# A fused retention and MLP kernel: two bursts of entry 2 taken together, and one scaling moved

## The chip, the cores and the metric

The kernel runs on one core of a Trainium2 chip. The metric is the device time of one execution in microseconds (us). The engines are named as in the profile: PE (TensorE matmuls), PEld (its weight loads), DVE (VectorE), ACT (ScalarE), POOL (GpSimd), SP (SyncE). Each engine runs its own queue in order; engines wait for one another by semaphores.

## The reference

Retention over 8 batch entries, 8 heads, 576 positions, 64 dimensions, and then an MLP with 2048 hidden units on the 4608 rows that come out:

```python
scores = (q @ k.T) / sqrt(64)
ret = scores * where(i >= j, gamma[h] ** (i - j), 0)   # gamma[h] = 1 - 2 ** (-5 - h)
x = (ret @ v)                                          # per entry and head
x = x.transpose(0, 2, 1, 3).reshape(4608, 512)
h = x @ w_in                                           # 512 -> 2048
out = (h * sigmoid(1.702 * h)) @ w_out                 # 2048 -> 512
```

q, k and v are loaded as bf16, sums are kept in f32.

## The kernel before

**Retention in steps.** Entry 0 is done on its own. Entries 1 to 7 are cut into 9 blocks of 64 positions, and three blocks make a step: `NWIDE` = 21 steps, m = 0 to 20, step m belonging to entry 1 + m // 3. So entry 2 has steps 3, 4 and 5, and step 5 has blocks 6 to 8. Heads 4 to 7 are shifted by 64 positions in k and v, so step 5 reads chunks 3 and 4 of the entry's five chunks of 128 positions.

A step needs two kinds of work on PE, all in 64x64 tiles. *In*: `score` (k times q of the step's blocks, L680) and `state` (sums of k times v, L666). *Out*: `values` (masked scores times v, L638) and `inter` (the running sums times q, L654). Between the two, DVE masks the scores into `sm` (`mask_wide`, L735), adds the sums to `zacc` (`state_wide`, L750 and L753) and a cast makes `zw` in bf16 of them, on DVE (L762) or on ACT (L759). After *out*, `evac_wide` (DVE, L724) multiplies by the decay and writes `xT`, the MLP's input.

`burst(m_out, m_in, cast)` puts *out* of one step and *in* of another on PE's queue at one place; either may be None. With both, the order is: one state, half of the values (the blocks of even number) with their `inter`, the scores, the other states, the second half of the values with theirs. The second half waits for PE's own first half. On DVE a burst queues `evac_wide(m_out)` first; with cast "DVE" then the mask, the sums and the cast; with cast "ACT" the sums, then the mask, and the cast is queued on ACT behind the next unit.

`step(m, into, cast)` is `burst(m, m + 1)` if `into` is true, else `burst(m, None)`; behind it `turn_step(m + 3)` queues transposing DMAs on SP (`turn_dma`, L572) that bring k and q of step m + 3 into `qk`, and from step 2 on loads are queued on POOL (L223, L236) for the entry three later. SP's queue also carries the DMAs of the output (L819).

`scale(m)` multiplies v by a decay factor on DVE (`scale_v`, L394): for step 3 chunks 0 and 1 of entry 2, for step 4 chunks 2 and 3, for step 5 chunk 4.

**The MLP in units.** 4608 rows make nine chunks of 512. For each, 16 units of `hidden` (four 128x512 matmuls, L771, then a GELU on ACT, L776) and 16 units of `project` (four matmuls, L804; the last of a row block is copied out by ACT, L813, and stored). Chunk 1 is done in two halves, with `hidden_half` (eight 128x256 matmuls, L788 and L794).

**The order** is written out by hand. `run(units, between)` queues the units in turn and behind unit i what `between[i]` holds. If a `step` stands behind a unit, the unit's matmuls wait, ahead of the first, for what the step's burst needs (`needs`); a `burst` named alone has no such effect. In the lines that change, `units_half(1, 1)` is 8 units, `units_o(1, (2, 3))` is 8, and `region(2, ...)` is chunk 2's 16 hidden and 16 project units.

Of the kernel before, what the change touches and what calls it, by code (L numbers as in the profile page):

```python
# [132 lines left out]
def bass_retnet_parallel__then__act_gelu_quick_kernel(  # L133
# [11 lines left out]
    with es:  # L145
# [469 lines left out]
        def needs(m_out, m_in):  # L615
            r = []
            if m_out is not None:
                b, cs = chunks(m_out)
                r += [("sm", si(m_out)), "zw"] + [("v", b % NST, c) for c in cs] + queries(m_out)
            if m_in is not None:  # L620
                b, cs = chunks(m_in)
                r += [(nm, b % NST, c) for nm in "kv" for c in cs]
                r += [("qk", (NC * b + c) % NQK, 1) for c in cs] + queries(m_in)
            return r
# [155 lines left out]
        def hidden_half(c, half, f, at, ahead=()):  # L780
            bank, key = at
            a0 = 512 * c + 256 * half
            toks = range(a0 // 64, a0 // 64 + 4)

            def fn(e):
                for i in range(2):
                    for a in range(4):
                        m = e.matmul(bank[:, 256 * i : 256 * i + 256],  # L788
                                     w_in_sb[:, a, 128 * (f + i) : 128 * (f + i) + 128],
                                     xT[:, a, a0 : a0 + 256],  # L790
                                     start=(a == 0), stop=(a == 3))
                return m
            R.op("PE", fn, r=[("w_in", f // 2)] + [("xT", x) for x in toks] + list(ahead), ps=[key])
            R.op("ACT", lambda e: e.activation(  # L794
                gT[c % 2][:, f : f + 2, 256 * half : 256 * half + 256],
                bank.rearrange("p (f n) -> p f n", f=2), AF.Gelu_apprx_sigmoid),
                w=[("gT", c % 2, f), ("gT", c % 2, f + 1)], ps=[key])
# [3 lines left out]
        def project(c, r, g, bank, key, eng="DVE", ahead=()):  # L801
            def fn(e):
                for f in range(4 * g, 4 * g + 4):
                    i = e.matmul(bank, gT[c % 2][:, f, 128 * r : 128 * r + 128], w_out_sb[:, f, :],  # L804
                                 start=(f == 0), stop=(f == NF - 1))
                return i
            R.op("PE", fn, r=[("w_out", g)] + [("gT", c % 2, f) for f in range(4 * g, 4 * g + 4)]
                 + list(ahead), ps=[key])
            if g == 3:
                m = ocount[0] % len(osb)  # L810
                ocount[0] += 1
                if eng == "ACT":
                    R.op("ACT", lambda e: e.activation(osb[m], bank, AF.Copy),  # L813
                         w=osb_keys[m], ps=[key])
                else:
                    R.op("DVE", lambda e: e.tensor_copy(osb[m], bank),  # L816
                         w=osb_keys[m], ps=[key])
                row0 = 512 * c + 128 * r
                R.op("SP", lambda e: e.dma_start(out[row0 : row0 + 128, :], osb[m]),  # L819
                     r=[("osb", m)], dma=("osb", m))  # L820
# [137 lines left out]
        def next_bank():  # L958
            turns[0] += 1
            return wide_banks[(1, 2, 0)[turns[0] % 3]]  # L960
# [44 lines left out]
        def run(units, between):  # L1005
            for i, unit in enumerate(units):
                ahead = []
                for fn, *args in between.get(i, ()):
                    if fn is step:
                        ahead += needs(args[0], args[0] + 1 if (len(args) < 2 or args[1])  # L1010
                                       and args[0] + 1 < NWIDE else None)
                unit(ahead)
                while later:
                    later.pop(0)()
                for fn, *args in between.get(i, ()):
                    fn(*args)

        def units_h(c):
            return [lambda ahead, f=f: hidden(c, f, next_bank(), ahead) for f in range(NF)]

        def units_half(c, half):
            return [lambda ahead, f=f: hidden_half(c, half, f, next_bank(), ahead)
                    for f in range(0, NF, 2)]

        def units_o(c, rows, eng="ACT"):
            banks = {}

            def unit(r, g):
                def go(ahead):
                    if g == 0:  # L1030
                        banks[r] = next_bank()
                    project(c, r, g, *banks[r], eng=eng, ahead=ahead)
                return go
            first = rows[:3]
            return ([unit(r, g) for g in range(4) for r in first]
                    + [unit(r, g) for r in rows[3:] for g in range(4)])
# [11 lines left out]
            {0: [(turn, 9, True), (scale_v, 8)], 1: [(burst, None, 1, "ACT")],  # L1048
             2: [(scale_v, 9)], 6: [(step, 1)]})
        run(units_o(1, (0, 1)), {3: [(scale, 3)], 5: [(step, 2, False)]})  # L1050
        run(units_half(1, 1), {2: [(burst, None, 3, "ACT")], 4: [(scale, 4)]})
        run(units_o(1, (2, 3)), {0: [(step, 3, True, "ACT")], 5: [(step, 4, False)], 6: [(scale, 5)]})

        def last_step(c):
            t = 512 * (c + 1) - 1 - S
# [2 lines left out]
        def region(c, at):  # L1058
            run(units_h(c) + units_o(c, range(4)), at)

        region(2, {2: [(burst, None, 5, "ACT")], 5: [(scale, 6)], 8: [(step, 5)], 13: [(scale, 7)],
                   17: [(step, 6)], 22: [(scale, 8)], 26: [(step, 7)]})
        for c in range(3, NCH - 1):
            steps = range(last_step(c) + 1, last_step(c + 1) + 1)
# [70 lines left out]
```

## Time and profile before

| | us |
|---|---|
| median of 3 runs | 297.17 |
| the 3 runs | 296.97, 298.06, 297.17 |
| time of the profiled execution | 296.6 |
| its span, first to last instruction | 294.8 |

All of a profile's times count from the span's start; the rest of the execution's time, 1.8 us, lies outside the span. A row of a timeline has start, length, engine, line, operation and count, and in brackets the idle time of the engine before it and what ended that. Chunk 1's last 16 units and the first of chunk 2, where the change is, lie between 65 and 92 us.

### The profile page before, as it was taken

What the parts mean: (1) busy time and instruction counts of PE and PEld (TensorE: products, weight loads), DVE (VectorE), ACT (ScalarE), POOL (GpSimd) and SP (SyncE); (2) the same over time, 40 slices, a digit from 0 to 9 for tenths busy, and PEclk for the clock granted to TensorE, in tenths of its full rate; (3) what the DMA queues carried; (4) which work ended last, traced back from release to release, by engine and by line L of the source; (5) the groups of instructions that cost most, each with busy time, mean ns of one, the idle gap of its engine ahead of it and who ended that gap; (6) DMA issues with size and microseconds to landing.
All of it is one profiled execution on the core that took longest, in us unless ns stands there. A gap on an engine that the chain in (4) does not pass through costs nothing.

```text
span 294.8 us, 7772 instructions
## 1 busy us (share of the span) xinstructions
PE 289.6 (98%) x3434; PEld 148.9 (51%) x3434; DVE 124.0 (42%) x221; ACT 126.6 (43%) x212; POOL 150.1 (51%) x202
## 2 busy tenths in 40 slices
PE   7999999999999999999999999999999999999996
PEld 3664556758544544554454544544444544444444
DVE  6899284644545443642424415235325504100012
ACT  7767338517175224531454045403650366036600
POOL 8958879999869879769968960000000000000000
PEclk9999999999999999999999999999999999999999
DMA  9999999999999999999999996008610200020012
GB/s 188 166 201 185 172 172 197 160 142 146 185 156 204 141 143 192 189 141 119 141 220 147 134 222 102 4 0 111 180 29 0 109 36 2 2 107 36 0 58 87
DMA packets 151746, 36.31 MB, mean 123 GB/s; under 512 B 141344, under 2 KB 147232, under 8 KB 151712
## 3 DMA queue, kind: packets, MB, share of 16 engines
q0 software_dynamic: 114224, 17.84, 90.9%
q1 hardware_dynamic: 37488, 17.97, 30.9%
q8 instruction: 27, 0.44, 0.6%
q14 instruction: 7, 0.06, 0.1%
HBM read 36.70 MB, written 9.44 MB: 157 GB/s over the span
## 4 chain that ended last, share of the span: by engine, by line
PE 93%; POOL 2%; DMA 2%; DVE 1%; issue 1%; POOLq 0%
PE psB L804 40%; PE psB L771 36%; PE psB L788 5%; PE psA L666 2%; PE psA L638 2%; DMA st_k<-in_k_dram 2%; PE psA L680 2%; PE psA L654 1%; PE psA L804 1%; PE psA L830 1%; POOL st_v L223 1%; POOL st_k L223 1%; PE psA L415 1%; DVE xT L557 0%; DVE sm L480 0%
## 5 line engine op out<-in xcount | busy, mean ns | idle before, releaser
L804 PE MATMUL psB<-w_out_sb,gT 128*128 128x512 bf16 x544 | 122.1, 379 | 0.0
L771 PE MATMUL psB<-xT,w_in_sb 128*128 128x512 bf16 x492 | 108.9, 379 | 0.0
L776 ACT ACTIVATE gT<-psB 128x512 bf16<-128x512 f32 x123 | 73.5, 597 | 38.7 <-PE psB L771 38.6
L804 PEld LDWEIGHTS psB<-w_out_sb,gT 128*128 128x128 bf16 x544 | 51.8, 98 | 60.3 <-DVE sm L735 0.4
L771 PEld LDWEIGHTS psB<-xT,w_in_sb 128*128 128x128 bf16 x492 | 47.4, 98 | 56.5
L724 DVE TENSOR_TENSOR xT<-psA,gq 128x768 bf16<-128x768 f32 x21 | 20.1, 957 | 113.9 <-PE psA L654 113.9
L236 POOL DMA_DIRECT2D st_k<-in_k_dram x70 | 52.9, 786 | 8.6 <-DMA st_k<-in_k_dram 3.0
L236 POOL DMA_DIRECT2D st_v<-in_v_dram x70 | 52.5, 779 | 4.5 <-DMA st_v<-in_v_dram 3.7
L813 ACT ACTIVATE osb<-psB 128x512 f32<-128x512 f32 x23 | 13.7, 597 | 71.9 <-PE psB L804 71.9
L223 POOL DMA_DIRECT2D st_q<-in_q_dram x36 | 32.3, 898 | 9.9 <-DMA st_q<-in_q_dram 6.0
L394 DVE TENSOR_TENSOR st_v<-st_v,vfac 128x512 bf16<-128x512 bf16 x38 | 24.8, 682 | 1.9 <-DMA st_v<-in_v_dram 1.9
L753 DVE TENSOR_TENSOR zacc<-zacc,psA 128x256 f32<-128x256 f32 x49 | 20.5, 418 | 7.5 <-PE psA L666 6.3
L735 DVE TENSOR_TENSOR sm<-psA,maskw 128x768 bf16<-128x768 f32 x21 | 19.9, 947 | 0.0
L788 PE MATMUL psB<-xT,w_in_sb 128*128 128x256 bf16 x128 | 15.0, 273 | 0.0
L816 DVE COPY osb<-psB 128x512 f32<-128x512 f32 x3 | 2.1, 691 | 29.7 <-PE psB L804 29.7
L788 PEld LDWEIGHTS psB<-xT,w_in_sb 128*128 128x128 bf16 x128 | 12.2, 98 | 1.7
L813 ACT ACTIVATE posi<-psB 128x512 f32<-128x512 f32 x8 | 4.8, 597 | 17.7 <-PE psB L804 17.7
L638 PE MATMUL psA<-sm,st_v 64*64 64x64 bf16 x504 | 11.7, 195 | 0.3
L666 PE MATMUL psA<-st_v,st_k 64*64 64x64 bf16 x448 | 11.8, 199 | 0.0
L666 PEld LDWEIGHTS psA<-st_v,st_k 64*64 64x64 bf16 x448 | 7.6, 105 | 8.3 <-issue 7.8
L794 ACT ACTIVATE gT<-psB 128x512 bf16<-128x512 f32 x16 | 9.4, 599 | 5.0 <-PE psB L788 5.0
L654 PE MATMUL psA<-qk,zw 64*64 64x64 bf16 x448 | 11.0, 194 | 0.0
(114 smaller groups left out, 172.2 us busy)
## 6 DMA issues: line engine op xcount, KB each, us to landing
out_dram<-osb SPq DMA_DIRECT2D x27, 256.0 KB, 4.2
st_k<-in_k_dram POOLq DMA_DIRECT2D x57, 64.0 KB, 6.7
st_v<-in_v_dram POOLq DMA_DIRECT2D x57, 64.0 KB, 6.5
st_q<-in_q_dram POOLq DMA_DIRECT2D x28, 128.0 KB, 7.9
w_out_sb<-in_moe_w_out_dram POOLq DMA_DIRECT2D x4, 512.0 KB, 11.3
out_dram<-posi SPq DMA_DIRECT2D x8, 256.0 KB
w_in_sb<-in_moe_w_in_dram POOLq DMA_DIRECT2D x3, 512.0 KB, 8.2
gT<-in_q_dram SPq DMA_DIRECT2D x2, 512.0 KB, 4.3
```

Of the source, the lines that this page charges most:

```text
L223: paced(R.op("POOL", lambda e, d=d, s=s: e.dma_start(d, s), w=[(nm, sl, c)], dma=(nm, sl, c), own=pace()))
L236: paced(R.op("POOL", lambda e: [e.dma_start(d, s) for d, s in parts], w=[(nm, sl, c)], dma=(nm, sl, c), parts=2, own=pace()))
L394: R.op(eng, lambda e: e.tensor_tensor(t, t, f, ALU.mult), r=[("vfac", min(b, 1))], w=[("v", sl, c)])
L666: i = e.matmul(psA[half(j), bank, off + 64 * t : off + 64 * t + 64], rows_of(st_k, m_in, g, u, h), rows_of(st_v, m_in, g, u, h), start=(t ...
L724: R.op("DVE", lambda e: e.tensor_tensor(xT[:, :, t0 : t0 + 192].rearrange("p (u j) n -> p u j n", u=2), psA[:, 2:4, 0:384].rearrange("p u ...
L735: R.op("DVE", lambda e: e.tensor_tensor(o, i, k, ALU.mult), r=["maskw"], w=[("sm", si(m))], ps=["S"])
L753: R.op("DVE", lambda e, to=to, src=src, was=was: e.tensor_tensor(to, was, src, ALU.add), r=[("zacc", (blk - 1) % 3)], w=[("zacc", blk)], p ...
L771: i = e.matmul(bank, w_in_sb[:, a, 128 * f : 128 * f + 128], xT[:, a, 512 * c : 512 * c + 512], start=(a == 0), stop=(a == 3))
L776: R.op("ACT", lambda e: e.activation(gT[c % 2][:, f, :], bank, AF.Gelu_apprx_sigmoid), w=[("gT", c % 2, f)], ps=[key])
L788: m = e.matmul(bank[:, 256 * i : 256 * i + 256], w_in_sb[:, a, 128 * (f + i) : 128 * (f + i) + 128], xT[:, a, a0 : a0 + 256], start=(a == ...
L804: i = e.matmul(bank, gT[c % 2][:, f, 128 * r : 128 * r + 128], w_out_sb[:, f, :], start=(f == 0), stop=(f == NF - 1))
L813: R.op("ACT", lambda e: e.activation(osb[m], bank, AF.Copy), w=osb_keys[m], ps=[key])
```

## The change

Before, step 4 is called with `into` false: its burst behind unit 5 of `units_o(1, (2, 3))` holds only step 4's values, and step 5's scores and sums have a burst of their own behind unit 2 of chunk 2, with the cast on ACT. After it, step 4 takes step 5's scores and sums in its own burst, with the default cast on DVE, and the burst in chunk 2 is gone. `scale(5)` goes from unit 6 of `units_o(1, (2, 3))` to unit 5 of `units_half(1, 1)`, behind `scale(4)`; counted in units that is nine units earlier, and eight ahead of the burst that reads it, where it was four ahead. Nothing else is edited: loads, turns and output DMAs keep their order in their queues.

```diff
-        run(units_half(1, 1), {2: [(burst, None, 3, "ACT")], 4: [(scale, 4)]})
-        run(units_o(1, (2, 3)), {0: [(step, 3, True, "ACT")], 5: [(step, 4, False)], 6: [(scale, 5)]})
+        run(units_half(1, 1), {2: [(burst, None, 3, "ACT")], 4: [(scale, 4)], 5: [(scale, 5)]})
+        run(units_o(1, (2, 3)), {0: [(step, 3, True, "ACT")], 5: [(step, 4)]})
...
-        region(2, {2: [(burst, None, 5, "ACT")], 5: [(scale, 6)], 8: [(step, 5)], 13: [(scale, 7)],
+        region(2, {5: [(scale, 6)], 8: [(step, 5)], 13: [(scale, 7)],
                    17: [(step, 6)], 22: [(scale, 8)], 26: [(step, 7)]})
```

## Prediction

> **What bounds the kernel now.** I read the page first (span, busy shares, shares of the chain), then the chain of waits in order of time, the waits by engine, and then the timelines of the engines around the place that changes, 62 to 92 us.
>
> ```profile
> span 294.8 us, 7772 instructions
> PE 289.6 (98%) x3434; PEld 148.9 (51%) x3434; DVE 124.0 (42%) x221; ACT 126.6 (43%) x212; POOL 150.1 (51%) x202
> PEclk9999999999999999999999999999999999999999
> ...
> PE 93%; POOL 2%; DMA 2%; DVE 1%; issue 1%; POOLq 0%
> ```
>
> PE is busy for 98% of the span and carries 93% of the chain that ended last; its granted clock is in the top tenth in every slice. PE's busy time is modelled, so the share alone proves little. What proves it is the rate: where nothing disturbs it, a 128x512 matmul follows the last one every 0.216 us.
>
> ```profile
> 278.55 10.36 PE psB L804 x48
> ```
>
> 10.36 / 48 = 0.2158. Whatever PE does beyond "matmuls x 0.216" in a stretch is what a burst or a stall costs. These are the waits that PE shows around bursts, from the view of waits (engine, line, releaser: us in total, times, longest):
>
> ```profile
> PEld psA L666 <- issue: 7.8, 20, 0.4
> PEld psA L638 <- issue: 1.7, 4, 0.4
> PEld psA L638 <- PE psA L654: 0.8, 4, 0.2
> ```
>
> Twenty bursts that begin with states (L666) and four that begin with values (L638) each open with 0.4 us in which no weight load runs, released by nothing that the profile shows. The four values-only bursts also wait once inside, 0.2 us, for their own first half (L654). No burst waits for a DMA. So a burst has a fixed price, and a values-only burst a second one. That is what the change removes once.
>
> **The bursts taken apart.** The timeline of PE, start and length in us, at the two bursts that become one, and at step 7, which has the same place in its entry as step 4 and already takes both halves in one burst (L666 opens it, L638 and L654 follow):
>
> ```profile
> 74.81 4.58 PE L804 MATMUL psB<-w_out_sb,gT 128*128 128x512 bf16 x20
> 79.31 0.26 PE L638 MATMUL psA<-sm,st_v 64*64 64x64 bf16 x8
> 80.09 1.90 PE L804 MATMUL psB<-w_out_sb,gT 128*128 128x512 bf16 x8
> 81.83 2.75 PE L771 MATMUL psB<-xT,w_in_sb 128*128 128x512 bf16 x12
> 84.51 0.26 PE L666 MATMUL psA<-st_v,st_k 64*64 64x64 bf16 x8
> 85.03 5.35 PE L771 MATMUL psB<-xT,w_in_sb 128*128 128x512 bf16 x24
> ...
> 100.04 7.94 PE L804 MATMUL psB<-w_out_sb,gT 128*128 128x512 bf16 x36
> 107.92 0.26 PE L666 MATMUL psA<-st_v,st_k 64*64 64x64 bf16 x8
> 108.81 1.47 PE L804 MATMUL psB<-w_out_sb,gT 128*128 128x512 bf16 x6
> ```
>
> Differences of starts give the lengths. Step 4's burst of values, 48 matmuls: 80.09 - 79.31 = 0.78. Step 5's own burst, 40 matmuls: 85.03 - 84.51 = 0.52. Step 7's joint burst, 88 matmuls of the same kinds: 108.81 - 107.92 = 0.89. Ahead of each, the large matmuls end late against their rate: 79.31 - 74.81 - 20 x 0.2158 = 0.18 ahead of step 4's; 84.51 - 80.09 - 20 x 0.2158 = 0.10 ahead of step 5's; 107.92 - 100.04 - 36 x 0.2158 = 0.11 ahead of step 7's.
>
> **The sum.** Matmuls neither go nor come: 48 + 40 = 88. Removed: 0.78 + 0.52 + 0.10 (the lead-in of the second burst). Added: 0.89. Net 1.40 - 0.89 = 0.51 us less on PE, which is the path. The lead-in of step 4's burst stays at 0.18, as what makes it longer than 0.10 stays (next part). By parts, the 0.51 is the wait inside the values-only burst (0.19) and one entry and exit (0.32):
>
> ```profile
> 78.33 0.56 PEld L804 LDWEIGHTS psB<-w_out_sb,gT 128*128 128x128 bf16 x4 [0.39 <-DVE sm L735]
> 79.31 0.14 PEld L638 LDWEIGHTS psA<-sm,st_v 64*64 64x64 bf16 x8 [0.42 <-issue]
> 79.74 0.21 PEld L638 LDWEIGHTS psA<-sm,st_v 64*64 64x64 bf16 x16 [0.19 <-PE psA L654]
> 84.51 0.14 PEld L666 LDWEIGHTS psA<-st_v,st_k 64*64 64x64 bf16 x8 [0.42 <-issue]
> ...
> 108.44 0.23 PEld L638 LDWEIGHTS psA<-sm,st_v 64*64 64x64 bf16 x16
> ```
>
> The last row is why I count the 0.19 as gone: in the joint burst scores and a state stand between the two halves of the values, and its second half shows no idle time in front.
>
> [...]
>
> **What the joint burst must wait for, and when that is there.** The wait is put ahead of the fifth unit of the projection, the load at 78.33 above, since a unit takes on the needs of the burst behind it. It already waits there 0.39 us for step 4's masked scores (L735), which costs PE some 0.08 us (0.18 - 0.10). Behind it in PE's queue is everything, so anything later than 78.33 is paid in full. New at this place are step 5's operands: keys and queries of chunks 3 and 4 turned, and chunk 4's v scaled.
>
> ```profile
> 68.42 1.20 SPq L572 DMA_TRANSPOSE qk<-st_k  x1
> 69.66 1.25 SPq L572 DMA_TRANSPOSE qk<-st_q  x1
> ...
> qk<-st_k SPq DMA_TRANSPOSE x1, 6.9
> qk<-st_q SPq DMA_TRANSPOSE x1, 6.4
> ```
>
> These are SP's ninth and tenth of the entry's turns, chunk 4's keys and queries, counted from the first turn at 52.8 us (the order of the code has ten for an entry); the lower rows are the view of DMA issues for the two (count, us from issue to landing). They land at 75.32 and 76.06, and the last is 2.27 us ahead of 78.33. Nothing in SP's queue moves.
>
> Chunk 4's v: its loads are issued at 63.17 on POOL, and the DMA view gives the later of the two 5.2 us.
>
> ```profile
> 63.17 1.40 POOL L236 DMA_DIRECT2D st_v<-in_v_dram  x2
> ...
> st_v<-in_v_dram POOLq DMA_DIRECT2D x1, 64.0 KB, 5.2
> ...
> 70.83 1.28 DVE L394 TENSOR_TENSOR st_v<-st_v,vfac 128x512 bf16<-128x512 bf16 x2
> 75.09 0.96 DVE L724 TENSOR_TENSOR xT<-psA,gq 128x768 bf16<-128x768 f32 x1 [2.98 <-PE psA L654]
> 77.20 0.95 DVE L735 TENSOR_TENSOR sm<-psA,maskw 128x768 bf16<-128x768 f32 x1
> 80.22 0.96 DVE L724 TENSOR_TENSOR xT<-psA,gq 128x768 bf16<-128x768 f32 x1 [2.07 <-PE psA L654]
> 81.10 0.68 DVE L394 TENSOR_TENSOR st_v<-st_v,vfac 128x512 bf16<-128x512 bf16 x1
> ```
>
> The later load starts at about 63.83 and lands at about 69.1. The scaling (0.68 us, now at 81.10) moves behind chunks 2 and 3's at 70.83: it runs 72.11 to 72.79, in the 2.98 us that DVE has empty before 75.09, and is done 5.5 us before PE asks. Its cost is nothing; the cover is those 2.98 us, and if it were gone each us of it would delay step 3's output (L724), then step 4's mask at 77.20 and so PE at 78.33, one for one.
>
> Behind the joint burst DVE now has step 4's output, step 5's mask, two sums and the cast of the sums to bf16, which ScalarE did before:
>
> ```profile
> 86.59 0.62 ACT L759 ACTIVATE zw<-zacc 128x512 bf16<-128x512 f32 x1
> ...
> 110.68 0.86 DVE L753 TENSOR_TENSOR zacc<-zacc,psA 128x256 f32<-128x256 f32 x2
> 111.58 0.43 DVE L762 CAST zw<-zacc 128x512 bf16<-128x512 f32 x1
> ```
>
> On DVE that cast took 0.43 at step 7. ScalarE loses 0.62, which was off the path. The output of step 4 is first on DVE, as before, 0.13 us behind the burst (80.22 against 80.09), and the next reader, the hidden layer at 81.83, stays two units (1.73 us) behind the burst; so it keeps its cover of 81.83 - 81.18 = 0.65. DVE's chain is done near 80.3 + 0.96 + 0.95 + 0.86 + 0.43 = 83.5; step 5's burst comes 24 matmuls behind 85.03, near 90.3, and asks for it one unit earlier, near 89. Cost nothing; cover 5 us.
>
> Bounds: the saving is at least 0 if all of it is taken up by a stall of 0.5 at the moved wait, and at most 0.51 + 0.08, if that stall went too. In the profiled execution the span goes from 294.8 to 294.3 and its time from 296.6 to 296.1. That execution is 0.57 under the median of the three runs shown, 297.17, so against the median I forecast **296.7 us**, 0.17% less. A measurement of this kernel can tell about 0.5%, 1.5 us, from no change, so this counts as the same.
>
> **Rivals.**
>
> *The turned queries come late (slower).* The joint burst asks 5.2 us earlier than step 5's own did (79.31 against 84.51). From a landing at 78.33 on PE stalls; from 78.84 the gain is eaten up; from 80.3 the time is over 0.5% longer. For it: the chain to that turn is long (load, then turn), and landings spread:
>
> ```profile
> DMA to landing us min/median/max: 2.4/6.9/8.3
> ```
>
> (all 60 turns). Against: with 8.3 in place of 6.4 the queries land at 77.96, still ahead. It takes a late load as well: were chunk 4's keys and the two turns behind them late by 4 us, and the last turn at its longest, it would land near 82, and the time would be 297.17 + (82 - 78.33) - 0.51 = 300.3. Chance 0.07, of which 0.04 beyond 0.5%.
>
> *The gain is taken back (no change).* PE comes 0.51 us earlier to step 5 and later to every step up to the end; if one of them had been held by DVE or a turn, the gain stops there: 297.2. Against: the only late lead-in I find from 60 us on is the 0.18 at step 4 itself; the others, as at step 7, are 0.10 or so, and PE shows no wait for a DMA at any burst. Chance 0.08.
>
> *Only the entry and exit go, and the inner wait stays:* 297.17 - 0.32 = 296.85. The row at 108.44 speaks against it. Chance 0.07. [...]
>
> **How the numbers follow.** The forecast has 0.76, the three rivals 0.22, and 0.02 is left for a gain beyond 0.5% that I can't name. Forecast and the last two rivals lie between 296.6 and 297.2; the three runs of before lie 0.2 below to 0.9 above their median, and a new median can fall within most of that. So the range is 296.1 to 297.8, with the late queries' worse part outside. Faster by over 0.5%: 0.02; within: 0.94; slower: 0.04.
>
> **What would show it.** Right: one burst of 88 matmuls near 79.3 us, opened by L666, about 0.89 long; between the large matmuls before and behind it no other burst until step 5's, which starts near 89.8 in place of 90.31; L666 with 20 waits of 0.4 still and L638 with 3; a DVE scaling near 72.1 with no wait for a DMA; a DVE cast near 83.1; all later starts 0.5 us earlier; PE still over 97% busy. Wrong: a lead-in over 0.3 ahead of 79.3, released by a turn or by L394; DVE waiting for a load near 72 us; a later lead-in over 0.2.

## The result, and the profile after

| | before | changed |
|---|---|---|
| median of 22 runs, us | 296.96 | 298.19 |
| lowest, us | 296.41 | 297.11 |

The changed kernel is slower, by about a third of a per cent: the ratio of the mean times is 1.0035 (95% interval 1.002 to 1.0051), and the medians lie 1.2 us apart. 0.5 us less was forecast. The execution profiled first took 304.55 us, with a stand of PE of 5.5 us in it and a stretch at a lower clock behind that, so sizes are taken from the second profile of the same kernel (297.94 us), and only the place from the first.

The page of the first one, engines, clock and chain:

```profile
span 302.8 us, 7736 instructions
PE 287.9 (95%) x3400; PEld 149.9 (50%) x3434; DVE 124.7 (41%) x222; ACT 126.1 (42%) x211; POOL 150.2 (50%) x202
PEclk9999999999959999999999999999999999999999
...
PE 90%; issue 4%; POOL 2%; DMA 2%; DVE 1%; ACT 1%; POOLq 0%
...
q8 instruction: 27, 0.44, 0.6%
```

Before, PE carried 93% of the chain and "issue" 1%. Now "issue", time in which the engine waited for nothing that the profile shows, has 4%, and one slice has half the clock. The last line stands in the page of before too. It is the DMA queue of the kind "instruction", and what follows leads to it: 27 packets, 0.44 MB, of 16 KB each.

The weight loads around the joint burst in the second profile (start, length in us; in brackets the idle time before and its releaser):

```profile
79.00 0.56 PEld L804 LDWEIGHTS psB<-w_out_sb,gT 128*128 128x128 bf16 x4 [0.49 <-DVE sm L735]
79.99 0.14 PEld L666 LDWEIGHTS psA<-st_v,st_k 64*64 64x64 bf16 x8 [0.42 <-issue]
...
80.51 0.30 PEld L638 LDWEIGHTS psA<-sm,st_v 64*64 64x64 bf16 x16
80.72 0.19 PEld L654 LDWEIGHTS psA<-qk,zw 64*64 64x64 bf16 x12
82.09 0.98 PEld L804 LDWEIGHTS psB<-w_out_sb,gT 128*128 128x128 bf16 x6 [1.18 <-issue]
```

The burst is as forecast: opened by L666, no wait inside, done within a microsecond. Ahead of it stands what stood there before, the wait for step 4's mask (0.49; 0.39 before), and no turn and no scaling of v. The new thing is the last row: behind the burst no weight load starts for 1.18 us, and nothing is named for it. On PE the gap is 1.30:

```profile
80.74 0.29 PE L654 MATMUL psA<-qk,zw 64*64 64x64 bf16 x12
82.33 1.67 PE L804 MATMUL psB<-w_out_sb,gT 128*128 128x512 bf16 x7 [1.30 <-issue]
```

The matmuls that wait (L804) belong to chunk 1's projection, whose operands were long there; the same matmuls follow step 4's burst without a pause in the kernel before. That speaks against an operand and leaves the instructions themselves. The DMA view of the same profile, by queue (packets, MB, share of 16 engines; over 100% as the times of packets overlap), for 75.1 to 79.9 us and then for 79.92 to 80.89:

```profile
q0 software_dynamic: 3766, 0.47, 154.2%
q1 hardware_dynamic: 1015, 0.54, 42.9%
...
q8 instruction: 1, 0.02, 6.2%
```

In the first stretch no packet of queue 8 runs. In the second there is one, from 79.92 to 80.89 by its record in the trace; PE goes on 1.20 us after it has landed. In the first profile the packet ran from 83.46 to 84.36 and PE went on at 86.00. And the gap falls at the same count of weight loads in both. The view of stretches, from 0 to within the gap (busy us and count of each engine), first for the second profile, then for the first:

```profile
0.00:81.50 81.50, 76.91 (x1096) 47.16 (x1106) 52.13 (x102) 43.99 (x73) 71.25 (x97) 1.00 1.80 172
0.00:85.00 85.00, 76.91 (x1096) 47.30 (x1106) 56.13 (x108) 43.73 (x73) 72.96 (x99) 0.99 1.76 171
```

The second count is PEld's: 1106 weight loads, whatever the time. The count alone proves little, for behind the 1106th weight load the joint burst ends: a wait of the matmul that follows it would stand at the same count. Only kernels in which the two come apart can tell (below).

The counts tell how many of PE's instructions go with a packet: 3434 weight loads and as many matmuls are 6868, 254 to each of the 27 packets; of the kernels below, the three shifted ones, with 7060 or 7062, have 28 packets, 252 to each, and the misplaced one, with 6980, has 27, 259 to each. In the trace of before the first packet begins behind 146 weight loads and the last behind 3364, 124 apart in the mean (3218 / 26). From these counts, 124 to 129 weight loads to a packet, I take it that some 128 with their matmuls use one up, an estimate; the joint burst alone is 88, in 0.9 us.

In what follows a *border* is the place in PE's stream where one packet ends and the next begins, and PE runs *dry* when it has used up all instructions that have landed. The *point* is the weight load 128 ahead of a border, one packet earlier, my estimate of where the next packet is asked for.

### The profile page after: what moved, and what is told of

Same layout as the page of the kernel before. It is cut to its first block, busy times and chain, and to the rows that moved or that the text cites. A ratio compares the mean times of both kernels' runs of the same rounds, so it can differ in the third digit from the quotient of the medians.

```text
span 302.8 us, 7736 instructions
## 1 busy us (share of the span) xinstructions
PE 287.9 (95%) x3400; PEld 149.9 (50%) x3434; DVE 124.7 (41%) x222; ACT 126.1 (42%) x211; POOL 150.2 (50%) x202
## 4 chain that ended last, share of the span: by engine, by line
PE 90%; issue 4%; POOL 2%; DMA 2%; DVE 1%; ACT 1%; POOLq 0%
PE psB L804 39%; PE psB L771 35%; PE psB L788 5%; PE psA L666 2%; DMA st_k<-in_k_dram 2%; PE psA L638 2%; PE psA L680 2%; PE psA L654 1%; PE psA L804 1%; PE psA L830 1%; POOL st_v L223 1%; POOL st_k L223 1%; PE psA L415 1%; DVE xT L557 0%; DVE sm L480 0%
## 5 line engine op out<-in xcount | busy, mean ns | idle before, releaser
L804 PE MATMUL psB<-w_out_sb,gT 128*128 128x512 bf16 x523 | 119.1, 382 | 8.4 <-issue 7.8
L771 PE MATMUL psB<-xT,w_in_sb 128*128 128x512 bf16 x481 | 107.8, 381 | 1.2 <-issue 1.0
L804 PEld LDWEIGHTS psB<-w_out_sb,gT 128*128 128x128 bf16 x544 | 52.2, 98 | 66.5 <-issue 7.1
L394 DVE TENSOR_TENSOR st_v<-st_v,vfac 128x512 bf16<-128x512 bf16 x38 | 24.7, 682 | 2.3 <-DMA st_v<-in_v_dram 2.3
L666 PE MATMUL psA<-st_v,st_k 64*64 64x64 bf16 x448 | 12.1, 199 | 0.3 <-issue 0.3
L666 PEld LDWEIGHTS psA<-st_v,st_k 64*64 64x64 bf16 x448 | 7.8, 105 | 8.7 <-issue 8.3
```

Source lines behind the costliest of these rows:

```text
L394: R.op(eng, lambda e: e.tensor_tensor(t, t, f, ALU.mult), r=[("vfac", min(b, 1))], w=[("v", sl, c)])
L666: i = e.matmul(psA[half(j), bank, off + 64 * t : off + 64 * t + 64], rows_of(st_k, m_in, g, u, h), rows_of(st_v, m_in, g, u, h), start=(t ...
L771: i = e.matmul(bank, w_in_sb[:, a, 128 * f : 128 * f + 128], xT[:, a, 512 * c : 512 * c + 512], start=(a == 0), stop=(a == 3))
```

## The experiments

The times are medians of 11 or 12 runs where not told otherwise, each beside runs of the kernel before on the same chip. The time up to step 3's own burst (the first L666 behind 66 us) varies, from 67.9 to 72.8 us over the profiles, so I also give for each profile the rest of the span from there (68.00 before) to its end. Before: 294.80 - 68.00 = 226.80.

**The changed kernel once more**, as it is. The text of its expectation names three theories, A (instruction supply), B (operands) and C (DVE), which the later ones go back to.

> The changed kernel once more, for a profile whose clock is not disturbed. Theory A (instruction supply): PE's instructions arrive in 16 KB packets (27 on queue 8 in both profiles), the joint burst uses 88 weight loads and 88 matmuls in 0.9 us at a place where the next packet has not landed, and PE stands behind the burst for about 1.7 us with nothing named as releaser; net +1.2 us, ratio 1.003 to 1.005. Theory B (operands): the turned queries or the scaled v of step 5 come late; then a gap of about 1.7 us stands ahead of the joint burst, ended by a turn or by L394. Theory C (DVE): the early scaling of v holds up DVE; then DVE's waits near 72 us show a load and step 4's mask ends later than 78.2.

298.05 against 296.79 us, ratio 1.0036 (1.001 to 1.0062). The gap is behind the burst, without a releaser; rest of the span 227.58. DVE does the scaling in one go with the two before it, no wait for a load:

```profile
71.39 1.89 DVE L394 TENSOR_TENSOR st_v<-st_v,vfac 128x512 bf16<-128x512 bf16 x3
```

So neither B nor C shows where it was expected: no turn and no L394 ends a wait ahead of the burst, and DVE waits for no load.

**The scaling alone.**

```diff
-        run(units_half(1, 1), {2: [(burst, None, 3, "ACT")], 4: [(scale, 4)]})
-        run(units_o(1, (2, 3)), {0: [(step, 3, True, "ACT")], 5: [(step, 4, False)], 6: [(scale, 5)]})
+        run(units_half(1, 1), {2: [(burst, None, 3, "ACT")], 4: [(scale, 4)], 5: [(scale, 5)]})
+        run(units_o(1, (2, 3)), {0: [(step, 3, True, "ACT")], 5: [(step, 4, False)]})
```

> The kernel before with the scaling of chunk 4's v moved and nothing else. Theories A and B: within 0.3 us of before (ratio 0.999 to 1.001). Theory C: most of the +1.2 us (ratio 1.003 or more).

297.03 against 296.79, ratio 1.000 (0.9981 to 1.0018); rest 226.78. The scaling costs nothing that these runs can show, and C falls.

**The stream shifted**, in the changed kernel and in the one before: 4 idle matmuls at the start give way to 100 small ones, so that every border falls 96 weight loads earlier in the work behind them. The first expectation below says that such matmuls warm PE up; what the trace of the kernel before shows is their pace: 0.43 us from start to start at first (1.59, 2.02, 2.44, 2.87), 0.22 or 0.23 from 5.95 on (5.95, 6.18; 8.81, 9.03, 9.25).

```diff
-        fill(9)
+        fill(5)
+        pad(100)     # 100 matmuls 64x64 of the idle tile
```

> The changed kernel with 192 more PE instructions at its very start: 4 of the 9 idle matmuls that warm PE up are replaced by 100 matmuls of 64x64 with their weight loads, in the time in which PE waits for the first k. Everything behind them is the same, but the borders of the 16 KB packets fall 192 instructions earlier in the stream, so that the packet in question is asked for earlier and the joint burst no longer ends where its predecessor ends. Theory A: the gap behind the joint burst goes and the time falls under before's by about 0.5 us (ratio 0.997 to 0.9995); what the start costs or gives is told by the run of before with the same start. Theories B and C: as the changed kernel, ratio 1.003 to 1.005, with the gap where it was.

> The kernel before with the same 192 instructions more at its start: the control for the start. All theories: within 0.3 us of before if the start is hidden (ratio 0.999 to 1.001); a difference here is what the start itself costs and is taken off the other run.

The changed kernel 297.02 (0.9999; 0.9982 to 1.0016), the one before with the same start 297.57 (1.0016; 0.9998 to 1.0035), both against 296.79: 0.55 us less with the joint burst, at equal starts (296.46 to 297.93 against 297.17 to 298.40, 11 runs each). Rest of the span 226.21 against 226.86, 0.65 less. The shifted changed kernel has no pause behind the burst:

```profile
80.25 0.14 PEld L666 LDWEIGHTS psA<-st_v,st_k 64*64 64x64 bf16 x8 [0.42 <-issue]
...
80.91 0.19 PEld L654 LDWEIGHTS psA<-qk,zw 64*64 64x64 bf16 x12
81.14 0.76 PEld L804 LDWEIGHTS psB<-w_out_sb,gT 128*128 128x128 bf16 x5
```

The two edits of the change and their operands are the same here as in the kernel with the gap; what is moved is the stream. The 1106th weight load is now a large one some 2 us ahead of the joint burst, and the packet landed 2.8 us before it. So the gap doesn't belong to the matmul behind the burst, which speaks against B, and this is the run that carries the cause. One thing changed beside the border: this packet landed 4.0 us after its point, not 5.8. With 5.8 it would still be 1.0 us early (78.00 - 71.20 - 5.8), where PE goes on 1.2 us or more after a landing; by this estimate little of the gap of 1.3 would be left. My claim that the ratio would fall under 1 missed: the start cost 0.8 us (step 3's own burst starts at 68.97 and 68.76 in place of 68.00).

**The kernel before, with the borders misplaced**: the same edit with `pad(60)`.

> The kernel before, joint burst not taken, with 112 more PE instructions at its start (4 of the 9 idle matmuls replaced by 60 of 64x64). By the counts of weight loads in the traces so far, PE ran dry 1106 weight loads into the stream; 56 more at the start put that point into step 4's burst of values, with the packet asked for 5.8 us earlier, as short as in the changed kernel (5.7). Theory A: the kernel before gets the gap that it never had, about 1.1 us with no releaser in or right behind step 4's burst of values, and stands about 1 us over the run of before with 192 instructions more (297.57), ratio 1.004 to 1.007 to before. Theories B and C: no gap there, 297.0 to 297.8.

A miss. 298.19 against 297.26 (1.0025; 1.001 to 1.0039), but most of the loss is at the start: step 3's own burst begins at 69.60, and the rest is 227.03. No gap stands at step 4:

```profile
80.95 0.14 PEld L638 LDWEIGHTS psA<-sm,st_v 64*64 64x64 bf16 x8 [0.42 <-issue]
...
81.72 1.19 PEld L804 LDWEIGHTS psB<-w_out_sb,gT 128*128 128x128 bf16 x7
```

The packet landed at 79.89, 4.3 us after its point, not 5.8, and 1.6 us before PE would have been dry. I had taken its latency for fixed. So no run has brought the gap about in a kernel without the joint burst.

**Fewer loads under way**, in both kernels: `AHEAD = 4` in place of 6.

> The changed kernel with 4 in place of 6 loads of POOL let under way at a time (the pace by which a load waits for the one so many before it). Theory A with the queue of loads as what holds the packet up: it lands about 1 us sooner after it is asked for (80.89 - 75.08 = 5.8 us in the run of the changed kernel), the gap of 1.2 us shrinks to 0.5 or less, and against its own control (the next run) it is 0 to 0.5 us faster. If the packet's lateness has nothing to do with the loads: the gap stays at 1.2 and it stays 0.8 to 1.3 us behind the control.

> The kernel before with 4 in place of 6 loads under way: the control. If loads come in time at this pace, within 0.5 us of before; where a later step waits for its operands, slower, and the other run with it.

300.33 and 299.63 (six runs each; ratios 1.0099 and 1.0097): both lose time early on (step 3's own burst at 70.20 and 72.80 us), and the difference of 0.7 is within their spread (298.65 to 301.11 and 298.98 to 301.61). The times decide nothing. The profile of the changed kernel says more: the packet lands 3.3 us after its point, and the gap is gone.

```profile
82.09 0.19 PEld L654 LDWEIGHTS psA<-qk,zw 64*64 64x64 bf16 x12
82.33 0.76 PEld L804 LDWEIGHTS psB<-w_out_sb,gT 128*128 128x128 bf16 x5
```

**The stream shifted at a later place**: the changed kernel with `pad(24)`, `pad(54)` and `pad(23)` in place of four of the idle matmuls between 7.5 and 11 us.

> The changed kernel with 194 more PE instructions, put at three places between 7.5 and 10.5 us where idle matmuls stood, instead of at the very start, where they cost both shifted kernels 0.8 us (297.57 against 296.79). Theory A: no gap behind the joint burst, and if the start is not hurt, 0.3 to 0.5 us under before: ratio 0.998 to 0.999, the fastest of all. If the start is hurt as much: 297.0, as the first shifted kernel. Theories B and C: 298.

296.95 against 297.26, ratio 0.9997 (0.9982 to 1.0012). No gap, rest 226.26, but the start lost 0.7 us again (68.70).

```profile
80.70 0.19 PEld L654 LDWEIGHTS psA<-qk,zw 64*64 64x64 bf16 x12
80.93 0.98 PEld L804 LDWEIGHTS psB<-w_out_sb,gT 128*128 128x128 bf16 x6
```

**The pace changed for a few loads only.** All loads keep 6 under way but the nine of entry 3's chunks 1 to 3:

```diff
+            back = 4 if 44 <= len(issued) <= 52 else AHEAD
-            return issued[-AHEAD] if len(issued) > 3 * NC - 2 + AHEAD else None
+            return issued[-back] if len(issued) > 3 * NC - 2 + AHEAD else None
```

> The changed kernel with 4 in place of 6 loads under way, but only for the nine loads of entry 3's chunks 1 to 3, which POOL issues from about 68 to 81 us and which stand in front of the late packet; all others at the old pace. Theory A: the packet lands some 3 to 4.5 us after it is asked for in place of 5.8, the gap behind the joint burst is under 0.4 us, no step waits for the nine loads, and the time is 0.2 to 0.5 us under before (ratio 0.998 to 0.9995). If the packet's lateness is not of these loads' making: gap 1.2, ratio 1.003 to 1.004. If these loads are then late for their steps: the gap is gone and another wait, ended by a turn or by L394, has come between 85 and 110 us.

> The kernel before with the same pace for the same nine loads: the control. It had no gap to lose: all theories 0.999 to 1.001, unless the nine loads come late for their steps, when it is slower by as much as the run beside it.

The changed kernel 297.20 (0.9997; 0.9982 to 1.0012), the control 296.78 (0.999; 0.9975 to 1.0004), both against 297.23. Half a success: 0.85 us under the changed kernel as it is, though on another chip, and still 0.4 us over its own control. The profiled execution (297.57) still has the gap, which the expectation had under 0.4, with the packet landing at 80.14 and 1106 weight loads done (one line was added above, so L805 here is L804 elsewhere):

```profile
81.67 1.41 PEld L805 LDWEIGHTS psB<-w_out_sb,gT 128*128 128x128 bf16 x8 [1.25 <-issue]
...
0.00:81.00 81.00, 76.81 (x1096) 47.13 (x1106) 51.81 (x102) 43.82 (x73) 68.91 (x93) 1.00 1.81 178
```

**The pace at 3**, for the same nine loads, and for 15 (`38 <= len(issued) <= 52`).

> The changed kernel with 3 loads under way for the nine loads of entry 3's chunks 1 to 3 (4 in the run before this one, where the packet landed 5.35 us after the request, still too late by a gap of 1.2 us in the profile, while the median fell by 0.85 us). Theory A: the packet lands 3 to 4.5 us after the request, the gap is under 0.4, ratio to before 0.997 to 0.9995. If the packet does not come sooner: gap near 1.2 and ratio 0.9995 to 1.003.

> The same with 3 loads under way from entry 2's chunk 4 to entry 3's chunk 3 (15 loads, issued from about 61 us). Theory A: packets 7 and 8 both land within 4 us of their request and no gap stands behind the joint burst; ratio 0.997 to 0.9995 if no operand comes late. If chunk 4's keys and queries of entry 2 come late by it: a wait ahead of the joint burst ended by a turn, or the gap, and 1.000 or more.

With nine loads: 296.59 against 296.75 (0.9993; 0.9977 to 1.0009). The profiled execution happens to be the slowest of its twelve, 298.44 us: the packet lands at 81.30, and PE stands 2.43 us at the same count. That is neither of the two outcomes expected.

```profile
82.69 1.41 PEld L805 LDWEIGHTS psB<-w_out_sb,gT 128*128 128x128 bf16 x8 [2.43 <-issue]
...
0.00:82.00 82.00, 78.15 (x1106) 47.46 (x1106) 53.53 (x103) 43.84 (x73) 67.19 (x92) 1.00 1.92 174
```

With 15 loads: 296.20 against 296.75, ratio 0.9986 (0.9968 to 1.0003), the lowest of all, though its interval still touches no change. The packet lands at 78.47, 4.0 us after its point, and the burst has no gap; rest 226.34. The kernel before was not run at a pace of 3; at 4 for nine loads it lay itself 0.45 us under the runs beside it, so this time can't be put down to the gap alone.

```profile
79.96 0.19 PEld L655 LDWEIGHTS psA<-qk,zw 64*64 64x64 bf16 x12
80.19 1.41 PEld L805 LDWEIGHTS psB<-w_out_sb,gT 128*128 128x128 bf16 x8
```

## Why the prediction was wrong

All profiles together. PE is or would be dry behind the 1106th weight load, and the point is 128 weight loads earlier. In the three shifted kernels the 1106th is a large weight load ahead of step 4's burst, in the others it lies in or behind a burst. The third column has the start of the 1106th weight load less the landing:

| kernel | packet landed after the point, us | 1106th start, less landing, us | gap on PEld, us | rest of the span, us |
|---|---|---|---|---|
| before | 5.8 | 4.3 | none | 226.80 |
| scaling alone | 5.4 | 4.7 | none | 226.78 |
| before, 4 under way for nine | 3.9 | 6.3 | none | 226.79 |
| before, misplaced | 4.3 | 1.6 | none | 227.03 |
| before, 4 for all | 3.9 | 6.3 | none | 226.84 |
| before, shifted | 3.1 | 3.7 | none | 226.86 |
| changed, first profile | 9.9 | -3.9 | 5.47 | 234.81 |
| changed, second profile | 5.8 | -0.1 | 1.18 | 227.58 |
| changed, 4 under way for nine | 5.4 | 0.2 | 1.25 | 227.48 |
| changed, 3 for nine | 6.8 | -1.1 | 2.43 | 228.65 |
| changed, 3 for 15 | 4.0 | 1.6 | none | 226.34 |
| changed, 4 for all | 3.3 | 2.1 | none | 226.64 |
| changed, shifted | 4.0 | 2.8 | none | 226.21 |
| changed, shifted later | 3.1 | 3.7 | none | 226.26 |

**The sum was right as far as it went.** The joint burst was forecast to save 0.51 us and to last 0.89. Its weight loads in the shifted kernel take 0.89, from 80.25 to 81.14. Where no gap stands, the rest of the span is 226.21, 226.26 and 226.34 with the joint burst (the two shifted kernels, and the pace of 3 for 15 loads) and 226.78 to 226.86 without it (before, scaling alone, shifted, pace of 4 for nine): 0.44 to 0.65 less. (With 4 under way for all it is 226.64 against 226.84, only 0.20, and the misplaced kernel has 227.03; why is open.) The inner wait of 0.19 is gone from the joint burst, and with it the rival in which it stays.

**The waits that it listed were costed rightly.** The turned queries and the scaled v were there, no wait of PE behind the burst is put down to DVE or to the cast. The late-queries rival did not happen, and where no gap stands the gain was not taken back at a later step.

**The step that failed is "what the joint burst must wait for".** It listed operands only. The term left out is the supply of PE's own instructions. In the kernel before, 40 of the 128 weight loads between the point and the dry place belong to large matmuls, and the stretch takes 10.1 us (5.8 + 4.3). The joint burst brings step 5's 40 small ones forward; now only 20 are large, 20 x 0.216 = 4.3 us less, an estimate that leaves 5.8, and 5.7 are measured (75.07 to 80.81). The packet and the start after it took 5.8 + 1.2 = 7.0. The difference, 1.3 us, is the gap of 1.30 on PE, as it must be within one profile; the check is that 1.30 - 0.51 = 0.79 is the growth of the rest of the span (227.58 - 226.80 = 0.78). The medians differ by 1.2 us, not 0.8: by the same sum the usual gap would be 1.7 us, an estimate, and profiles show it from 1.2 to 2.4, and 5.5 once. The share of each size was not measured.

**The evidence lay open before.** The page of the kernel before has these lines:

```profile
DMA  9999999999999999999999996008610200020012
...
q8 instruction: 27, 0.44, 0.6%
```

A packet of that queue ran from 79.40 to 80.36 us, just beside the burst, on DMA engines that every slice up to there shows as busy. I read "PE shows no wait for a DMA at any burst" as "no DMA can hold PE up"; in these profiles the wait for instructions is listed as "issue", with no releaser named. The three rivals were about late operands, a gain taken back and the inner wait, and the price of being dry for a microsecond was in none. The range ended at 297.8, below what the gap costs.

What holds the packet up is not shown, only that it is late. At the old pace it landed 5.4 to 5.8 us after its point in three profiles of the unshifted stream and 9.9 in a fourth, but 3.1 to 4.3 in the shifted and misplaced kernels. With fewer loads under way it took 3.3 to 4.0 in four profiles, but 5.4 and 6.8 in the two of the changed kernel with 4 and 3 for nine loads. So the load traffic ahead of the packet may matter, and it is not all; whether the instruction packet stood behind other transfers, and behind which, no trace here resolves.

The point itself is an estimate, for no record shows when a packet is asked for. The starts of the packets bear it out: at the seven points from 850 to 1618 weight loads (every 128), in all 14 profiles, none of these packets begins before its point, and the earliest begin 3 to 18 weight loads behind it (18 to 52 behind in the kernel before).

## What to carry to other kernels

Small matmuls use up instructions fast: the joint burst takes 88 weight loads and 88 matmuls in 0.9 us, a time in which four large matmuls run (4 x 0.216). Count PE's instructions per microsecond, not only its busy time, before two dense bursts are put close together, and look where the instruction packets land in the DMA view. An idle stretch put down to "issue" that begins at the same count of instructions in each execution, ends soon after a packet's landing, and goes when unused instructions are put in front, points to a wait for instructions. Here another place in the stream removed it in both kernels tried, fewer loads under way in two of four.

## What was not expected of the hardware

PE stood at one count in four profiles of three kernels, behind the 1106th weight load, at 80 to 81 us, for 1.18, 1.25, 2.43 and 5.47 us. It went on 1.2 to 1.6 us after the packet's landing (80.89 and 82.09; 80.14 and 81.67; 81.30 and 82.69; 84.36 and 86.00), also where the packet had landed shortly before PE was dry (80.14 against 80.32). The longest of these stands:

```profile
86.00 0.13 PEld L804 LDWEIGHTS psB<-w_out_sb,gT 128*128 128x128 bf16 x2 [5.47 <-issue]
```

After it the granted clock (third number from the end) was 0.50 in the stretch from 85 to 90 us and back at 1.00 from 95 us on, in this one profile:

```profile
85.00:90.00 5.00, 3.59 (x9) 1.46 (x11) 0.00 (x0) 0.96 (x2) 3.77 (x6) 0.50 1.92 157
95.00:100.00 5.00, 4.84 (x115) 2.66 (x114) 0.80 (x1) 2.64 (x5) 5.00 (x8) 1.00 1.86 201
```
